# Attention and a gated feed-forward layer on one core: a V bank from the common pool, fifteen exponential tiles, a new instruction order, and a DMA queue kept in program order

## The chip, the cores and the metric

The kernel runs on one core of a Trainium2 chip. The core has TensorE (PE, matrix products into eight PSUM banks), VectorE (DVE), ScalarE (ACT), GpSimd (POOL), and SyncE (SP), which issues all the DMAs here. The metric is device time in microseconds (us) of one execution. Before the change it is 1711.22 us, the median of 3 runs (1711.19 to 1714.54). One more execution was profiled.

## What is computed

The reference, cut to its core (2048 tokens of width 512, 32 heads of width 16, a hidden width of 1792, all in float32):

```
xn = layernorm(x)
q, k, v = split(xn @ wqkv)                  # 32 heads of 16
s = softmax(q k^T * 16**-0.5) v  @ wo       # full attention
g = silu(((xn @ w_gate) * (xn @ w_up)) @ w_down)
return x + s * g
```

## The kernel before

**Attention** is cut into 32 units: a group of 4 heads by a chunk of 512 queries. A unit has 16 turns of 128 keys. For each unit the scores are formed twice. The first time (`score`, L927) queries lie on the partitions, and DVE reduces each 128x512 tile to row maxima (`mx`, L929). `maxima` and `rest` turn these into two extra rows of the query operand (through `MD` in DRAM back to `qs`). The second time (`expo`, L955) keys lie on the partitions, the extra rows subtract the maximum, and ACT takes the exponential into a tile `e` (L957). A turn gives four `e` tiles. `pv` (L966) then multiplies these by `V` into one PSUM bank that holds the unit's whole sum; `heads` transposes it on DVE (code `x`, L993), scales it (`c`), transposes it back and stores it to `OD` (`b`).

**The projections, the feed-forward layer and the output projection** are sums of 12 or 15 products (an `Out`). Operands are split into a high and a low part, so that three products stand for one in higher precision.

**Halves.** A score product has 48 or 50 rows, and each product of an `Out` is cut into two of 64 rows (L465). One lies on partitions 0 to 63, the other on 64 to 127, and two of these "halves" run at once on the two halves of the array. `pv` instead uses all 128 rows and 32 columns, four heads side by side. So PE changes between two ways of use: a stretch of halves, then a **V block** of one, two or three turns, then halves again.

**The order** of PE, ACT and DVE is written by hand in the string `ORDER`. `t`, `T` are halves for exponentials (lower, upper rows), `s`, `S` halves for maxima, each with the digit of its PSUM bank; `o` opens an `Out` in a bank, `f` and `F` are its lower and upper halves; `v`, `w`, `z` are V blocks of one, two and three turns; `l` is a tiny read by ACT after a lower half sum; `e` and `d` are evacuations of an `Out` by ACT and DVE; `X` and `k` transpose and copy tokens at the start; `m`, `r`, `x`, `c`, `b`, `h`, `y` are the steps named above and of the feed-forward layer; `Q` loads and splits attention output for the output projection. The part before `|` is the start.

**Banks.** Seven PSUM banks (digits 0 to 6) are shared by the halves through tags; the eighth, tag `pv`, belongs to `pv` alone, and a unit's first turn takes it again only when the previous unit's transposition has read it.

**Tiles.** The `e` tiles are a ring of `EBUFS` = 14. The raw copies `qr` in the early pool are a ring of 3.

**DMAs.** SP runs its DMAs in the order in which it is given them; a DMA whose data or target isn't ready holds all that are behind it. Up to `|` they are in program order, and after it the framework's scheduler orders them. `wdr` is one buffer through which parts of `w_down`, of `wo` (four, at the last feed-forward sum) and of `OD` pass to POOL to be split. In the last stage `z_out` makes output rows: it loads 512 KB of `YD` (the gate) and 512 KB of `x` into one of two "side" tiles (`hh` and `dl`) for two sums at a time, when the first of these opens; `end` (L796, L797) multiplies and adds, and stores to `out`. `kept_back` is a list of DMAs that are written a given number of `Out`s later.

Of the kernel before, what the change touches and what calls it, by code (L numbers as in the profile page):

```python
# [1129 lines left out]
```

## Time and profile before

| | |
|---|---|
| median of 3 runs | 1711.22 us |
| the profiled execution, its own time | 1711.76 us |
| span of the profile, first to last instruction | 1708.6 us |
| POOL busy | 583.7 us |
| weight loads (PEld) busy | 1089.4 us |
| DMA engines, mean busy share (queue q1) | 28.9% |
| moved by DMA | 145.80 MB, mean 85 GB/s |

The span leaves out 3.2 us of the execution that lie around the first and the last instruction. A row of the timeline gives the start, the duration, the engine, the line, the tiles (output<-inputs) and xN for the number of records merged in the row. Each `pv` product leaves two records, so a turn of four products is x8, and V blocks of one, two and three turns are x8, x16 and x24. In the groups by line the columns are busy time and mean duration, then the idle time of the engine ahead of the group and what ended it.

### The profile page before, as it was taken

How to read it: one execution, taken by the hardware profiler on the slowest of the kernel's cores; microseconds unless marked ns; L12 is line 12 of the kernel's file. 1: busy time of each engine (PE TensorE's matmuls, PEld its weight loads, DVE VectorE, ACT ScalarE, POOL GpSimd, SP SyncE). 2: the span in 40 equal slices, each digit the busy share in tenths (PEclk: the TensorE clock that was granted, in tenths of full speed). 3: DMA queues.
4: the chain of work that ended last, by engine and by line, in shares of the span. 5: the costliest groups of instructions: out<-in, count | busy, mean ns of one | idle time of the engine just before them, and what ended most of it. 6: DMA issues, size and time to landing. Idle time of an engine off the chain costs nothing.

```text
span 1708.6 us, 35418 instructions
## 1 busy us (share of the span) xinstructions
PE 1695.8 (99%) x13792; PEld 1089.4 (64%) x13792; DVE 1440.7 (84%) x2464; ACT 1221.5 (71%) x2503; POOL 583.7 (34%) x618
## 2 busy tenths in 40 slices
PE   8999999999999999999999999999999999999998
PEld 6976666666666556666666666666666666665555
DVE  7788888888898988888898888888988888888942
ACT  6257777777767777777677777776777677677783
POOL 6433334413504155053131622423235234043531
PEclk9999999999999999999999999999999999999999
DMA  6357332412223122321124211321225111022442
GB/s 207 112 205 230 146 131 98 103 29 60 61 50 83 64 84 72 53 75 48 42 94 84 87 40 42 82 56 53 84 70 113 30 60 53 22 80 71 134 129 79
DMA packets 119794, 145.80 MB, mean 85 GB/s; under 512 B 12620, under 2 KB 74060, under 8 KB 116940
## 3 DMA queue, kind: packets, MB, share of 16 engines
q1 hardware_dynamic: 119628, 143.55, 28.9%
q8 instruction: 108, 1.77, 0.4%
q14 instruction: 58, 0.48, 0.1%
HBM read 95.94 MB, written 47.45 MB: 84 GB/s over the span
## 4 chain that ended last, share of the span: by engine, by line
PE 97%; DVE 1%; POOL 1%; issue 0%; DMA 0%; ACT 0%; POOLq 0%; SPq 0%; DVEq 0%
PE b L465 37%; PE pv L966 27%; PE b L955 16%; PE b L927 15%; PE v L354 1%; PE p L354 0%; DVE mx L929 0%; DMA ks<-in_x_dram 0%; POOL dh L770 0%; PE b L332 0%; POOL y L441 0%; PE xT L317 0%; POOL hl L769 0%; ACT ks L295 0%; POOLq L1122 0%
## 5 line engine op out<-in xcount | busy, mean ns | idle before, releaser
L929 DVE TENSOR_REDUCE mx<-b 128x1 f32<-128x512 f32 x2048 | 1278.3, 683 | 186.4 <-PE b L927 99.3
L957 ACT ACTIVATE e<-b 128x512 f32<-128x512 f32 x2048 | 1084.1, 603 | 362.8 <-PE b L955 194.2
L927 PE MATMUL b<-ks,qs 48*128 48x512 f32 x2048 | 751.6, 412 | 0.0
L955 PE MATMUL b<-qs,ks 50*128 50x512 f32 x2048 | 722.4, 414 | 0.2
L966 PE MATMUL pv<-e,V 128*32 128x512 f32 x4096 | 488.4, 598 | 0.0
L955 PEld LDWEIGHTS b<-qs,ks 50*128 50x128 f32 x2048 | 342.4, 184 | 159.4 <-issue 48.6
L927 PEld LDWEIGHTS b<-ks,qs 48*128 48x128 f32 x2048 | 357.5, 184 | 131.6 <-DVE mx L929 51.0
L966 PEld LDWEIGHTS pv<-e,V 128*32 128x32 f32 x4096 | 109.0, 109 | 233.5 <-issue 223.6
L465 PE MATMUL b<-fh,w1h 64*128 64x512 f32 x504 | 199.4, 398 | 0.4 <-ACT look L500 0.4
L465 PE MATMUL b<-fl,w1h 64*128 64x512 f32 x504 | 197.4, 394 | 0.0
L465 PE MATMUL b<-fh,w1l 64*128 64x512 f32 x504 | 197.1, 393 | 0.0
L247 POOL CAST w1h<-w1r 128x512 fp32r<-128x512 f32 x60 | 36.6, 610 | 468.3 <-DMA w1r<-in_wg_dram 261.5
L465 PE MATMUL b<-fh,w0h 64*128 64x512 f32 x500 | 196.4, 395 | 0.0
L465 PE MATMUL b<-fl,w0h 64*128 64x512 f32 x500 | 195.7, 393 | 0.0
L465 PE MATMUL b<-fh,w0l 64*128 64x512 f32 x500 | 195.5, 393 | 0.0
L465 PE MATMUL b<-dh,hh 64*128 64x512 f32 x448 | 160.8, 396 | 0.0
L465 PE MATMUL b<-dh,hl 64*128 64x512 f32 x448 | 158.2, 394 | 0.0
L465 PE MATMUL b<-dl,hh 64*128 64x512 f32 x448 | 157.3, 393 | 0.0
L247 POOL CAST w0h<-w0r 128x512 fp32r<-128x512 f32 x60 | 36.6, 611 | 206.3 <-DMA w0r<-in_wu_dram 109.0
L465 PEld LDWEIGHTS b<-fh,w1h 64*128 64x128 f32 x504 | 92.9, 185 | 11.2 <-issue 2.2
L465 PEld LDWEIGHTS b<-fh,w1l 64*128 64x128 f32 x504 | 93.1, 185 | 8.8 <-issue 3.4
L465 PEld LDWEIGHTS b<-fl,w1h 64*128 64x128 f32 x504 | 93.3, 186 | 5.1 <-issue 0.8
(153 smaller groups left out, 1988.1 us busy)
## 6 DMA issues: line engine op xcount, KB each, us to landing
w1r<-in_wg_dram SPq DMA_DIRECT2D x56, 256.0 KB
w0r<-in_wu_dram SPq DMA_DIRECT2D x56, 256.0 KB
wdr<-in_wd_dram SPq DMA_DIRECT2D x56, 256.0 KB
qs<-QD SPq DMA_DIRECT2D x64, 192.0 KB
ks<-KD SPq DMA_DIRECT2D x12, 768.0 KB
KD<-hl SPq DMA_DIRECT2D x16, 512.0 KB
QD<-hl SPq DMA_DIRECT2D x16, 512.0 KB
OD<-tr SPq DMA_DIRECT2D x31, 256.0 KB
```

The lines of the kernel that those rows point to most:

```text
L247: cast = nc.gpsimd.tensor_copy(hi, raw)
L354: nc.tensor.matmul(o, l(d), r(d), start=k == d == 0, stop=k == 2 and d == ND - 1)
L465: nc.tensor.matmul(self.o, l[rows], r[rows], start=x == 0 and n == 0, stop=last and (x == 0 or self.engine is not None), skip_group_check= ...
L927: nc.tensor.matmul(o, QS[i][b:b + KB, pr, t * P:(t + 1) * P], k[b:b + KB, pr, kc * 512:(kc + 1) * 512], start=True, stop=True)
L929: nc.vector.tensor_reduce(MX[i][:, j, t, kc:kc + 1], o, axis=AX.X, op=OP.max)
L955: nc.tensor.matmul(o, k[b:b + KR, pr, kt * P:(kt + 1) * P], QS[i][b:b + KR, pr], start=True, stop=True)
L957: fst["recent"] = fst["exp"] = nc.scalar.activation(e, o, AF.Exp, scale=DH ** -0.5).ins.name
L966: nc.tensor.matmul(fst["pv"][32 * j:32 * j + 32], V[:, kt, h0:h0 + 32], es[j], start=kt == 0, stop=kt == NT - 1)
```

## The change

- `EBUFS` goes from 14 to 15.
- The bank of a unit's V sum is taken from the common pool, now eight banks (digits 0 to 7), by a new code `P` with its digit. A new unit's bank can be taken while the old one is still unread, so a V block may hold turns of two units.
- `ORDER` is new from its first line to its last.
- `order_.run(rest_of)` moves inside the context that keeps SP's queue in program order.
- The load of a side tile is put off by one `Out` (`kept_back` with 1). Of the four raw parts of `wo`, two go through the weight tiles `w1r` and `w0r` at once, and two through `wdr` one and two `Out`s later.
- The ring `qr` has 2 buffers; copies of turned tokens at the start use up to four `e` tiles instead (`turned_raw`).

No product, evacuation or transfer of data is added or taken away: 512 turns, 9508 halves, 218 `Out`s in both.

```diff
-EBUFS = 14
+EBUFS = 15
 ORDER = """
-X01o2fkX34kffkfS5fS6jfffjfS0ffS5ko1lX36jfFfFjfFfFs0FkfFfFfFufFfS5fFfFo4Fls0kX35fFfFefS0fFfFfFfFfFs0FfFfFkfFo6S2lfFfFef
+X01o2S3X45kkfS6fS7kfS0fS1fjfffjfffko4lX36jfFfFjfFfFfFkfFs7FufFfFfFfFfFo0S1lfkfS7fFfFfFfFefFfFfFfFs1FfFo5FlfFfX36efFfFkf
...
+    spare = []
+    def turned_raw():
+        if now[0]:
+            return qp.tile([P, D], F32, name="qr", bufs=2)
+        if len(spare) < 4:
+            spare.append(etile())
+        else:
+            spare.append(spare.pop(0))
+        return spare[-1]
...
-        raw = qp.tile([P, D], F32, name="qr", bufs=3)
+        raw = qp.tile([P, D], F32, name="qr", bufs=2) if hi is None else turned_raw()
...
+                elif code == "P":
+                    pvs[len(pvs)] = pool(int(next(codes)))
...
-                for d in range(ND):
-                    raw = fp.tile([P, D], F32, name="wdr", bufs=1)
+                def part(d, raw):
                     dma(raw, wo[d * P:(d + 1) * P])
                     split_rows(raw, *[t[:, d] for t in fst["w"]])
+                for d, n in enumerate(("w1r", "w0r")):
+                    part(d, wtile(n).rearrange("p d q -> p (d q)"))
+                for d in (2, 3):
+                    order_.kept_back.append([d - 1, lambda d=d: part(d, fp.tile([P, D], F32, name="wdr", bufs=1))])
...
         def begin():
             if t % 2 == 0:
-                here = fst["side"][t // 2]
-                assert not sides[t // 2]
-                dma(here[:, 0:2], YD[c][:, t:t + 2])
-                dma(here[:, 2:4], x[(4 * c + t) * P:(4 * c + t + 2) * P].rearrange("(t p) d -> p t d", p=P))
-                sides[t // 2] = 2
+                order_.kept_back.append([1, load])
+        def load():
+            here = fst["side"][t // 2]
...
     def pv(i, kt, es):
         g = i // NC
-        if kt == 0:
-            fst["pv"] = fst["banks"].tile([P, 512], F32, tag="pv", name=f"pv{i}", bufs=1)
         for j in range(4):
             h0 = (4 * g + j) * VW
-            nc.tensor.matmul(fst["pv"][32 * j:32 * j + 32], V[:, kt, h0:h0 + 32], es[j],
+            nc.tensor.matmul(pvs[i][32 * j:32 * j + 32], V[:, kt, h0:h0 + 32], es[j],
                              start=kt == 0, stop=kt == NT - 1)
...
             with tc.manual_schedule(engines=SPLITS):
                 order_.run(begin)
-        order_.run(rest_of)
+            order_.run(rest_of)
```

Where one unit ends and the next begins, PE's order before the change, at the second of these places (x4 is one turn; `pv_2476` is the old unit's sum, `pv_3186` the new one's):

```order
L966 MATMUL pv_2476<-e,V 32x512 x4
L955 MATMUL b_3161<-qs,ks_132 128x512
L955 MATMUL b_3165<-qs,ks_132 128x512
L955 MATMUL b_3169<-qs,ks_132 128x512
L465 MATMUL b_3068<-fh,w1h 128x512
L927 MATMUL b_3174<-ks_132,qs 128x512
L465 MATMUL b_3068<-fl,w1h 128x512
L955 MATMUL b_3178<-qs,ks_132 128x512
L955 MATMUL b_3182<-qs,ks_132 128x512
L966 MATMUL pv_3186<-e,V 32x512 x8
```

PE's order after the change at the third of these places, which is of a kind that the order before doesn't have (L986 is `pv`, L949 `score`, L977 `expo`, L477 a half of an `Out`; `b_3138` and `b_3845` are the V banks of two units):

```order
L977 MATMUL b_3836<-qs,ks_132 128x512
L977 MATMUL b_3840<-qs,ks_132 128x512
L986 MATMUL b_3138<-e,V 32x512 x4
L986 MATMUL b_3845<-e,V 32x512 x4
L949 MATMUL b_3863<-ks_541,qs 128x512
```

Before, two turns of two units stood in two blocks with eight halves between them; after, they stand in one block. Counted over PE's whole order, the 512 turns stand in 236 V blocks before (40 of one turn, 116 of two, 80 of three) and in 211 after (13, 95, 103).

SP's order before the change, in the last stage around the second refill of a side tile (`dl<-YD_123`); `OD_120` is attention output of the second chunk of queries, `OD_122` of the fourth:

```order
L177 DMA wdr<-OD_120 128x1x512
L177 DMA hh<-YD_123 128x1024
L177 DMA hh<-in_x_dram 128x2x512
L177 DMA dl<-YD_123 128x1024
L177 DMA dl<-in_x_dram 128x2x512
L177 DMA w1r<-OD_122 128x1x512
```

SP's order after the change, from the second refill to the third (`hh<-YD_124`):

```order
L177 DMA OD_120<-tr 128x512
L177 DMA wdr<-OD_120 128x1x512
L177 DMA dl<-YD_123 128x1024
L177 DMA dl<-in_x_dram 128x2x512
L177 DMA out_dram<-dl 128x512
L177 DMA w1r<-OD_122 128x1x512
L177 DMA w0r<-OD_122 128x1x512
L177 DMA wdr<-OD_122 128x1x512
L177 DMA wdr<-OD_122 64x1x512
L177 DMA out_dram<-dl 128x512
L177 DMA hh<-YD_124 128x1024
```

The second refill now stands behind a store of `OD_120` and a load of what was just stored, and the third behind four loads of `OD_122` of which the last two pass through the one `wdr` buffer.

More of the change, by code (lines that the diff above doesn't have):

```diff
@@ new lines @@
+FfFfS7fFfFo2S4lefS6fFfFfFs0FfFs7FfFfFmfFfFfS4fFo1S6lfS0fFfFefFfFfFrs7FfFfFs4FfFs6S0fFfFo3FlfS7efFfFs4FfFfFfFs6S0fS7fS5
+fFfFfFo2FlfFfFfFes4Fs6Fs0FfFfFs7Ft1S5fT4fFfFfT6fFfFs0Flo1es7T4t6FfFs5Ft3S0fFt4FfS7t6FfS5fT3fFs0FfT4fS7fT6fFfFs5Flt3T4s
+0Fs6FP7wet3S5t4Fs0Fs6Ft2Fs3Ft5Fo4Ft0FfFfS2fT6fS5fT3fFfS0fT6s2Fs5T3vet6S0t3T1s2S5ws0T6fS2fT3fo1S5lfT6fT0s3Ft2FfFs6Ft5Fs
+0FfFt3FfS2fT6fFs5Ft3FfS0fFfS2efS6s5T3lzs0T4s2Ft3Ft6Fs5Ft4Fo0FfFt3S2fFt6Ft5FfS4fFfS2fT3fFfS6fS4efT5ms2T3wrs6T1s4T5t3T2v
+fS6t1T5ls4S3vt2S6o1T5fS4fFfT3fS2t6Fs5Ft4FfFs3FfT2s6Ft5FfS4fFt2T3fFfFfFs6S5lt2S4wes6T3t2Fs5Ft0Fo4FfS3fT6fS2t5FfFs0FfT3s
@@ new lines @@
+6FfT2fS5fFt3FfFfFfS0et2T6ls5S3P1zxs0T2s5Fo6T3fFt7Fs2Ft0FfFs5FfT3s7FfT2fFs0Ft3FfS5fT7fS2fFfS0efT3t5S7lwcs2T4o3S0fT5fT7f
+FfS4t2FfFs0FfT5s7Ft4FfFfS2t5Fs0Ft7S4fFfFs2FfS5es0T7lzs4T6o2T7fS5fFt0FfS6fT4s7FfFt5S0fFfT6fS4t7Fs5FfFt0T6fFs4Fs7FfFt0T5
+lwebt6S4o7Fs0T5t3FfFfS6fS4t5FfT0fFfS3t6Fs5FfS4t0FfFfT3fFms6Ft0T5fFs4S3lzers6T0t5Fs4Fo2Ft3Fs0FfFs6T5fT4s3FfFfT0s5Ft6FfF
+fS4fFfS3efT0fS5fT6t4S7lwt0S3t6Fo5S7t4FfFs0Ft3Fs6Ft7FfFfS4fT0s3FfT6fS7fFfT0fFfS4s3T6fFt0S7lzext6S4o3S7fT0fS1fT2fFs4T6fF
+fT0s7Ft2Fs1FfFt6FfS4t0FfS2t7Fs6FfS1fT0t4FlP7zcs2Fs6Feo0T4fFs1FfT5fFs2T4fFfT6s5Fs1Ft4FfFt2S6fFt5FfFfS4fS1efT2s6T5lwt3S4
@@ new lines @@
+t2Fs1Fs6Ft5Fo3Ft4FfS2fT1fFfS5t6FfS4t2FfS1fFfT6fFfFbfS5es4T2ls1T6ws5T0s4Ft2Ft6Fs1Ft0Fo5FfS2fFfT4fS6s1T0fFfT2s4FfFt0S6fF
+fS1fFfS2et0T4lzmrt3S6o1S2fT0fFfT4s3FfT6fS0fT2s4FfFt3Fs6Ft0FfFs2Ft3FfFfFfS4et0T6ls2S3wt5S4t0Fs2Ft6Fo3FfS5t4FfS0t2FfFs6F
+fT5fS4fT0s2FfFfT5fFfFs6S4efS0s2T5lzs6T1s4Ft5Ft0Fs2Ft1Ft6Fs5Fo4FfS0fFfT2fS1fT5fS6fFt2T0fFfS1fS5fFt2T6lP0wexs1T2o5T6fS7f
+FfT3fS2fT1fFfS7fT6s3Ft2FfFs1Ft6Fs7Ft3Fs2FfFt6T1fFs7S3lzecs2T6s7T1o4FfFt3Fs6FfFs2T1fFfT7s3Ft6FfS1fFt2S7fFt3S6fFfFfS1efT
+2s7T3lwt5S6o1S7fT2fT3fFs5FfFt6S2t7FfS3fFt5FfS6t2FfFs7FfT3fFs5Ft2S6fFs7T3lzebs5T2s6Ft3Ft4Fo7Fs2Ft5FfFs6FfT3s4FfS2fT5fFf
@@ new lines @@
+T3fS6fT4fFfS5t2T3fFms6S4lwers5T2o3S6t1Fs4FfFt2Fs5Ft1FfFfT6s2FfT4fFs5FfT1fS6t2FfFfS4fT1fS5t6S2lwdt1S4t6Fs5Ft2Fo7FfS1t4F
+fFfS5fT6s2Ft1FfS4fFt6T5fFhfS2fFs1Fs4S6zext5S2fS1fT3o4S6lfT0fS5fT2fFt3FfS1t0FfFt2Fs6FfT3fFs5T0fS1fFt2FfFs6Flt3Fs5S0t1FP
+2zcdht3S6o5S0fT1fFt7FfS3fT6fFt1Fs0FfT7s3Ft6FfFs1FfT0s7FfFfS3efT6s1T0lws7T4s3Ft6Fo0Ft1Fs4FfFt7FfS3fT6s1Fs4FfT7fFfFfT6fS
+3t7S1fFfS4fT6zlbdht7S3s1Ft6Ft4Fo5Fs7FfT3s6FfFfT1fS4fT7fS3t6Fs1FfFt4FfS7fFfS3efT6s1T4lwmrt0S7o6S3t4FfFt1Fs0Ft7FfFfS3fT4
+fS1fFfT7fS0s3T4fFfT1fFs7Flt0Fs4Fs3T1zdhs7T0s4Ft1Fs3Ft5Fs0Ft7Ft1Fo4FfFfS5fT3fS7fT0fFfS1t3S5fFfFfS7efT0s1T3lws5T6t0Fs7Fs
@@ new lines @@
+1Ft3Ft6Fo5FfFs7FfT0fS3fFfT6fS1t0FfS7fT3fS6fFt1S0fFt7S3lP6zdhxs0T1o7S3fT4fT2fFfS1fFs0T4s3Ft2FfFt1FfS4t0FfFs2FfT3s1FfFs4
+FfS0et3S2lwct5S1o4T3fS0fT2fFfS5t1Ft3FfS0fFt2Fs5FfT1fFfT3s0FfT2fS5fT1fFs3FfFs0S2ls5Ft1Fzds3T1s0Ft2Ft5Ft7Fs1Fo3FfS2fT0fF
+fT5s1FfT7fS2fT0fFfS5t1FfS7t2FfFfS0t5Ft1Fs7S2zebs0T5fT1fS7o4lfT2fS5fT0fFt1Fs7Ft2FfS5t0FfFms1Ft7Fs2Ft5FfFfFfS0fT7s1FfT5f
+FfFfS2es0S7lzrs1T5t3Fs2Ft0Fs7Ft5Fo1Fs3Ft2FfT0fFs7FfFt5S3fT2fFfS0s7FfT5fT3fFfS2fT0fS5fS7s3Ffet2T0lzxs5T4t2Ft0T7s3Fo6Fs4
+FfFfT5fS2fT3fS0fFt7FfS4t5FfS2t3Fs0Fs7FfT4fFs5Ft2FfFht3S0lP4zect2S7s5T3o0T1fFfFfS2t7Fs3Ft5FfS1fFfT2s7FfT3s5FfFt2T1fFs7S
@@ new lines @@
+3fFfFt2S5lwes7T1o3T2fS5fFfT6fS1fT7fFfS5fT2s6Ft1FfFs7Ft2Fs5Ft6FfFs1Ft2S7fFt5S6lzbdht2S1t5S7o6T0fFfFfS2fT1fS5fFfT7fS0fT2
+s1Ft5Fs7FfFt0FfFs2Flt5Fs1Fs7T0wemrs2T5o1Fs7T0fFt3Fs5Ft2Fs0Ft7FfFfS3fT5fFfS0fT2fS7s3T5fFfFt2T0fFs7S5lzdht2S3o0T7fS5fFfS
+6t2FfFs3T7fFt5Fs2Ft6Fs7FfT3fFs5FfT2fFfFfS7et6T3ls5S2wt1S7t6Fs5Fs2Ft3Fs1Ft7Fo6FfT5fFfS3s2T7fFfFfT5fS1fT7s3FfFfT5fS2s1T7
+lP3zdhxs2T5t7Fs1Ft0Fo4Fs5FfT2fFfS1fT7fS0t5FfFs2Fs1T7fFt0FfFfS5fS2efT7s1T0lcwt6S5t7Fs2Fo0Ft1Fs6Ft5FfS7t2FfFs1Ft6FfFfS7f
+T5fS2fT6fS1fFfT5fS7t2S6lzdhs1T5t2Fs7Ft6Fo4FfS5fT1s2Ft7FfS6fFt5FfS1t2FfFs7FfT5fFfS6fS1efS2t5T7lwbt0S6o1S2fT5fFfT7fS0fT6
@@ new lines @@
+fS5fT2fFfS7fT0s6Ft5FfS2fFt0T7fFs6Fs5FfFs2Fls0Fms7Ft6Fzdrs5T6o2T0fS7fT4fFfS6fT5fS0t7FfFfS4t6FfFt5S0t7FfFt6S4fFs5T0fFfFs
+4T7fFs6Fls5Fs0Fs4T7zds6T7t5Fs0Ft4Ft1Fs7Fo6FfT5fT0fS4fFs7Ft1FfFt5FfS4t0Ft7FfS1fFfFfT5dfS4fS0fT7fS1s2T5lP4zxs0T7t5Fs1Ft2
+Ft3Fs7Fs0Fo5FfT1fFfS2fT7fT3fS0fS1fFt7S2fFfFt3T0fFfS1fS7cfFt3Flt2Fs0S1zdt3S7t2Fo0S1fFfT6s3FfT7s2FfT1t6FfFs3Ft7Fs2FfFt1F
+fS6fT3s7FfT2fFs1Ft6T3fFhs7S2lzdt6S1o3Fs7T2fFfT5fS6t1FfFfS7fT2fS5t6Fs1FfFt2Fs7FfT5s6FbfFs1T2fFs7T5lwems6T2o5T0fS1fS7fFt
+2FfS6t0FfT1fFfS2t7Fs0Ft6FfS1fFt2Frs7FfFs0T6fFt2S1lzdhs7T6t2Fs0Ft1Fo3FfS6t7FfFs0Ft2Fs1FfT6fS7fFfT2fS0t1S6fFfFfS7efS2t1T
@@ new lines @@
+0lwt5S6o1Fs7T0fFt2Fs5FfFs6T0s7FfT2fFfT5fS0fT6fS2fFt7FfFs5Ft6T0fFs2S7lP5zdhxs2T6s7Ft0Fs3Ft4Ft6Fo2FfFfS7t0FfS4fT3fFfS6fT
+0fS7t4FfFfS3s6T0fFt7S4lwect0S3s6T7t1Fo4FfFs0FfT3fFs6Ft7Fs1FfFfT3s0Fs6T7fFfFs1T3wdhs0T7t3T6s1S2vs0T7fS1s3T6vt7S2fT6fS0f
+S1o3lfT7fS2t6FfFt0FfS7t1FfS6t2FfT0fFfS7fT1s6FfFt2Fbs0Ft7FfS1ms6Flzdrs0T2o7S1fT6fFfS4fT2fFs0T6fFt1Fs2Ft4FfS6fFt0S1fFt2F
+s4FfFt0S6fFs1T2lwds4T0t2Fs6Ft1Fs3Fo0FfT4s2FfFt6Fs1Ft3FfS4fT2fS6fFfT1fFfT3dfS4fS2s6T1lws7T3t1Fs4Fo2Ft6Fs3FfS7t1FfT4fFfS
+6t3Ft1Fs7FfFfFfT4dfS6fT3fS7fT1s0S4lP3zyxt1S6o7T0s4FfFt5Fs1FfFt6Fs4T0fFfS5fFfT6fS1s4T0fFt5FfFfFs1S6efS0t4T5lwct2S1s6Ft4
@@ new lines @@
+Fs0Ft5Fs2Fo1FfT4fFs6T5fFt0FfS4fFt5FfFfT2dfS6fS0fT5fS4t7S2lzyht5S6o0T7fS4fT2fFfS5fT6fS7t4FfFt2FfS5fT6s7Ft4FfFs2Fs5FfFs7
+Fls6Ft4Ft2Fwebs5T4o7S6fT2fT1fFs4FfT5fFmfT2s6Ft1FfS4fFt5FfS2t6FyfFs1Ft5S4zrdht6S2fS1o5T4lfS0ffT6fS2t4FfFt1FfS6t0Fs4FfT2
+s1FfFt6Fs0FfT4fFfS2t6Fls1Fs4T0wyet6S2o0T7s1FfFt4Fs6FfT2s7Ft1FfFfS4fT6fS2fT7s1FfFfT6fFs4Fs2T7fFt6S1lP4zdhxt7S2o6S1t5FfT
+3fFs7FfFfT2fS1t5FfS3fFt2S7fFt1FfS5fT3fFs2Flt7Fs1Fs5T3wect7S2o1S5fT3fFs0FfT7fFs2T3fFt5Fs7Ft0Fs3FfT2fFfS5fT7s0FfFs3T2fFs
+5T7lzdhs0T2o3T7fS5fFt6FfS2fT0fFs5Ft7Fs6Ft2Fs0FfFt7S5fFs6T2fFfFfS0efT7t2S5lwbt1S6o7S0fT2fFfT5fS1fT6fFs0Ft2Fs5FfFt6S1fFt
@@ new lines @@
+2S0fFfFs5T6fFt1Fls2Fmzdhrt6S0t1Fo5S2t3FfFfS6fT0fFs2FfT1s3Ft6FfFs0Ft1Fs2FfT3fS6fFfS0efT1s2T3lws6T7s0Ft1T3o2FfFfS7fT6fS1
+t0FfFs3Ft7S6fFt1FfS0fFt7S3fFfT6s1FfFfT7fS0t6S3zdxs1T7fT6o0S3lfT5fS4fS7fT1fFt6Fs3Ft5Fs4Ft1FfFs7Ft6Fs5FfT3fFfS4t1FfS6t7F
+fFfFfS5efS3cs4T1lP7zs6T2o5T1fT3fS4fFfS2fT6fFfT1fS4t3FfFs2Ft6Fs1Ft4Fs3FfFt6Fs2Ft1FfFs4FfS3efT6t2S1zfS4o0T6lfS3fT2fT1fS4
+fFt6Fs3Ft2Fs1Ft4FfFs6Ft3FfS2t1FfFs4FfT3fS6fT2bfFfFfFs4S1les3T2t6Fzs4T5s1Ft2Ft6Fs3Ft5Fs4Fo2FfT1fFfS6s3T5fFfT4fS1fFs6T5f
+Ft3S4fFmfFt5S1fFhs3S6lzert5Fs4T0o1FfFfT3s6T5fFfT4s0FfFt3Fs6Ft5FfFfS0fT4s3FfFfS6efT5s0S4lwt2S3o6S0fT5fFt4FfS2fT3fS5t0Ff
@@ new lines @@
+Fs4Ft2Ft3FfS5fFs0Ft2S4fFfFt3T5fFt2S0lwdhxs4T3s0Fo5T2fFs1T7fFt3T4fFs2Fs0FfFt7T1fFs3FfFfS2t4T7fFfS0fS3fFs1S4leP2zct7S0t6
+Ft3S1o4FfFt7FfS0fFfT6t1FfS3fFfT7s0FfT6fFs3FfT1s7FfFs0T6lwdht1S3o7S0t6FfFfT5fS1fT3fFfS0fT6s5FfT1fFs3Ft6Fs0Ft5FfFs1Fs3Ff
+S6et0S5lzbs1T4s3Fo0T6fFt5Fs4Ft1FfFfS3fT6s5Ft4FfFs1Ft6FfFfT3dfT4fS5fS1fS6s7T3lwht4Ft3S5o1FfS6t7FfFmfT4fT5s3Ft6FfS7fFfFt
+4FfS3t5FfS7fFs6FfS4et3T5lwrs7T0s6Fo3T5fT4fFs0FfT7s5FfT6fFs4FfT0fFfS5t7S6fFt0S4fFfFt7Fls5Ft6S0zdht7S4o5S0fT6fFfFt7S1fFt
+4FfS0t6FfS7fT1fFs4FfT0s6Ft7FfFs1Ft0T4fFs6S7lP1wext0S6s7Fo4T3fFfS2fT0fFfT6s7Ft3Fs0FfFfT2s6FfT7fS3t0FfS2fFfT6fFfS7t0S3lF
@@ new lines @@
+cs2S6zds7T0t3Fs2Fs6Ft5Ft0Fs7Ft3Fo2FfFfT5fS6fT0fS7fT3fFfT5s6FfFs7T0fFt3FfS5fT6fS0s7FfS3zlds5T6t0Fs7Ft3Fo4FfS6fT5fFfT0bf
+S7fT3fT6fFfFs5Ft0FfS7t3FfFs6Ft5FfS0t7T3fFfFs6S5lzdmrs0T7t3Fs6Ft5Fs2Fo7Fs0FfT3fFt6FfS5fT2fS3fS0t6FfFfT5fFfS2t6S3fFt0S5f
+FfFt6FfS2s3T0lzds5T6s2Ft0Ft3Fs4Fo6Ft5FfS0fS2fT3fFfT4s5Ft0FfFs3Fs2T4fFs5T0fFfFt4FhfS3s2T0zdxt4S5fS3o0T2lfS7fT1fT4fS5fFs
+2Ft3Fs1Ft7Ft4FfFs5FfFt3Fs2FfT7s1FfS4fS3efT5P7wlct6S2t5Fs1Ft4Ft3Fs6Fo2Fs5FfT1s4FfFfT6s3FfT5fFfFfT1dfS4fT6fS3fS5t1S0lzht
+6S4o3S5t1Ft0FfFfS6t4Fs1FfS5fT0fFfT6s4FfFs1T0fFs5T6fFfFs4T0fFs1T6lwebs5T0s4Ft6Fo1FfS2t0FfFs5T6fFfT4fS0t2FfS6fFt5FfS4t0F
@@ L163 @@
+fFfFfFfFfFo4FlfFfFfFdfFfFfFfFfFfFfFfFwlxFFFcFbFFFFF
 """
@@ L334, in copy @@
         def copy(half, o):
-            raw = qp.tile([P, D], F32, name="qr", bufs=3)
+            raw = turned_raw()
             nc.scalar.activation(raw, o, AF.Copy)
@@ L364, in qk_proj @@
         yield from full(o, ((hi, lambda d: xh[c][:, d]), (lo, lambda d: xh[c][:, d]), (hi, lambda d: xl[c][:, d])))
-        hi, lo = qp.tile([P, D], F32R, name="hl", bufs=2), qp.tile([P, D], F32, name="qr", bufs=3).bitcast(F32R)
+        hi, lo = qp.tile([P, D], F32R, name="hl", bufs=2), qp.tile([P, D], F32, name="qr", bufs=2).bitcast(F32R)
         nc.scalar.activation(hi, o, AF.Copy)
@@ L974, in heads @@
         tn = tr.rearrange("p b e -> p (b e)")
-        pv_bank = fst["pv"]
+        pv_bank = pvs[i]
         late = i >= NU - NC
```

197 lines of the change are left out of this document (71 added, 126 removed).

## The prediction

> **What bounds the kernel now.** I read the page first (busy times, slices, chain), then the windows by stage, then PE's timeline at single blocks.
>
> ```profile
> span 1708.6 us, 35418 instructions
> PE 1695.8 (99%) x13792; PEld 1089.4 (64%) x13792; DVE 1440.7 (84%) x2464; ACT 1221.5 (71%) x2503; POOL 583.7 (34%) x618
> PEclk9999999999999999999999999999999999999999
> PE 97%; DVE 1%; POOL 1%; issue 0%; DMA 0%; ACT 0%; POOLq 0%; SPq 0%; DVEq 0%
> 0.00:50.00 50.00, 44.36 (x299) 34.66 (x301) 34.96 (x86) 30.67 (x58) 33.52 (x44) 1.00 0.59 192
> 500.00:550.00 50.00, 50.00 (x415) 30.95 (x414) 44.61 (x76) 35.75 (x75) 18.20 (x19) 1.00 0.45 88
> ```
>
> The last two rows are windows: the stretch, its length, then the busy times of PE, PEld, DVE, ACT and POOL, the granted clock, the DMA share and GB/s. PE is busy all the time but for some 13 us (1708.6 less 1695.8), of which 5.6 lie in the first 50 us; its granted clock is full; the chain of waits runs through PE for 97%. The end therefore moves only if PE's own stream gets shorter or new waits get into it. But "busy" hides how densely PE issues. That is seen at a V block:
>
> ```profile
> 117.03 0.44 PE L955 MATMUL b<-qs,ks 50*128 50x512 f32 x1
> 117.05 0.41 PE L927 MATMUL b<-ks,qs 48*128 48x512 f32 x1
> 117.40 1.92 PE L966 MATMUL pv<-e,V 128*32 128x512 f32 x16
> 119.25 0.50 PE L955 MATMUL b<-qs,ks 50*128 50x512 f32 x1
> 119.25 0.49 PE L927 MATMUL b<-ks,qs 48*128 48x512 f32 x1
> 119.59 0.40 PE L955 MATMUL b<-qs,ks 50*128 50x512 f32 x1
> 119.59 0.39 PE L927 MATMUL b<-ks,qs 48*128 48x512 f32 x1
> 119.82 0.39 PE L955 MATMUL b<-qs,ks 50*128 50x512 f32 x1
> ...
> 109.19 2.78 PE L966 MATMUL pv<-e,V 128*32 128x512 f32 x24
> 111.91 0.50 PE L927 MATMUL b<-ks,qs 48*128 48x512 f32 x1
> ```
>
> A pair of halves starts 0.23 us after the pair before it (119.59 to 119.82). A three-turn block takes 2.72 us from its start to the next pair (109.19 to 111.91), a two-turn block 1.85 (117.40 to 119.25): a turn costs 0.87 and each block about 0.11 beside its turns. Ahead of the block 0.35 pass instead of 0.23 (117.05 to 117.40), 0.12 more; the first pair behind it takes 0.34 instead of 0.23 (119.25 to 119.59), 0.11 more. So **each change between halves and a V block and back costs PE about 0.35 us** on top of its work, and all of it lies on the path.
>
> **The change, part by part.**
>
> *Fewer V blocks.* Work is the same; the order has 211 blocks instead of 236. 25 x 0.35 = **8.8 us less**. Nothing else needs to happen for this: it is PE's own time. With 0.01 us of reading error in each of the three terms it is 8 to 9.6.
>
> *The banks and the fifteenth tile.* They cost no instruction. Three-turn blocks need twelve full `e` tiles ahead of them, so what could go wrong is that ACT or DVE can't follow.
>
> ```profile
> L929 DVE TENSOR_REDUCE mx<-b 128x1 f32<-128x512 f32 x2048 | 1278.3, 683 | 186.4 <-PE b L927 99.3
> L957 ACT ACTIVATE e<-b 128x512 f32<-128x512 f32 x2048 | 1084.1, 603 | 362.8 <-PE b L955 194.2
> ```
>
> Both engines' idle time is mostly waiting for PE: 363 us ahead of ACT's exponentials, 186 ahead of DVE's maxima, 0.79 per block of the 236. DVE has the smaller reserve and it lies in the V blocks, where no scores are made; it is a rival below. Small waits between halves exist already: from 111.91 to 117.05 there are 44 halves, so 22 pairs and 21 steps, in 5.14 us; with 0.34 for the first step and 0.23 for the others they would take 4.94. So 0.2 us are lost in such a stretch, some 40 us over the some 200 long ones of the run. I take that as unchanged by the new order, with a tenth of it, 4 us, as the bound to either side.
>
> *The start.* Copies of turned tokens go through spare `e` tiles instead of `qr`. The PE idle time of the first 50 us is 5.6 us and lies in the start that the change leaves alone (the loads, the layer norm and the first transpositions). I take nothing; 1 us either way bounds it: POOL, which splits the copies, is busy for 33.5 of the 50 us there (the fifth of the busy times in the row), so it has a third of the time in reserve.
>
> *`wo` in two ways, `wdr` freed.* Two parts no longer wait for the one buffer. PE isn't shown waiting for them, so nothing.
>
> *SP in program order, later refills.* Up to the last stage the waits at SP are for things that were given out shortly before, and loads stand far ahead of use; nothing. In the last stage two refills of a side tile stand behind waits. The rows on which I price them:
>
> ```profile
> 1608.84 0.71 DVE L993 STREAM_TRANSPOSE tr<-pv 128x512 f32<-128x512 f32 x1
> ...
> 1611.24 0.23 DVE L980 RECIPROCAL rc<-tr 128x16 f32<-128x16 f32 x1
> 1611.51 0.42 DVE L981 TENSOR_TENSOR on<-tr,rc 128x256 f32<-128x256 f32 x1
> 1611.97 0.71 DVE L985 STREAM_TRANSPOSE tr<-on 128x512 f32<-128x512 f32 x1
> ```
>
> ```profile
> 1612.71 0.32 SPq L177 DMA_DIRECT2D OD<-tr  x1
> 1615.69 0.60 SPq L177 DMA_DIRECT2D wdr<-OD  x1
> 1616.34 0.58 SPq L177 DMA_DIRECT2D w0r<-OD  x1
> 1621.97 6.65 SPq L177 DMA_DIRECT2D wdr<-OD  x2
> 1629.34 0.34 SPq L177 DMA_DIRECT2D out_dram<-dl  x1
> ...
> 1662.51 0.39 SPq L177 DMA_DIRECT2D dl<-YD  x1
> ```
>
> ```profile
> 1665.00:1666.00 1.00, 1.00 (x10) 0.68 (x7) 0.00 (x0) 0.19 (x1) 0.00 (x0) 1.00 1.06 279
> 1666.00:1667.00 1.00, 1.00 (x9) 0.81 (x6) 0.00 (x0) 1.00 (x3) 0.17 (x1) 1.00 0.58 197
> 1667.00:1668.00 1.00, 1.00 (x11) 0.42 (x13) 0.00 (x0) 1.00 (x3) 0.92 (x2) 1.00 0.01 4
> ```
>
> A refill from `YD` issued at 1662.51 has landed when the traffic ends at about 1666.9: 4.4 us. *Second refill* (`dl<-YD_123`): from the V block's end, DVE's four steps take 0.71+0.23+0.42+0.71 = 2.1, the store of `OD` issues, the load of what it stored issues 3.0 later (1612.71 to 1615.69) and takes 0.6 to issue: the refill goes out 5.7 to 5.8 us after the block and lands at 10.2. DVE's `end` for it stands 42 halves and one two-turn block after: 42 x 0.117 + 1.85 + 0.35 = 7.1, and 0.4 for the last product: DVE waits 2.7. *Third refill*: the four loads of `OD_122` need 1.2 for the first two and 6.65 for the pair through `wdr` (the row of that length), the stored row 0.4 and the refill lands 4.4 later, 12.7 us behind `Q3`. `end` stands 47 halves, one two-turn and one three-turn block behind: 5.5 + 2.2 + 3.1 = 10.8. DVE waits about 1.9. Behind both waiting instructions stand DVE's maxima, whose banks PE needs; and DVE has 0.79 us of idle time per block in which to catch up. So PE loses between nothing (all is absorbed) and 4.6; I take the middle, **2.3 us more**. The other refills have waits of nothing or a few tenths by the same sum.
>
> [...]
>
> *Sum*: 1711.76 (the profiled execution's own time) - 8.8 + 2.3 = 1705.3. That execution is 0.5 us above the median of the runs shown, so **1704.7 us** for the median.
>
> **The rivals.**
>
> *A. DVE keeps its idle time.* DVE is 89% busy in the window of 500 to 550 and nearly without a pause between the V blocks. A three-turn block starves it longer. If its 186 us of idle time don't shrink with the number of blocks, DVE is the bound and gives all back at the banks: 1711. For it: longer blocks, the same seven banks to fill ahead of most of them. Against: DVE would have to lose 0.88 per block instead of 0.79, and one more bank is to be had where units change.
>
> *B. Slower by the queue.* The place is the last stage. If the refills land 5 us or more behind their `end` at three places, and the score rows of the last unit (`MD`) stand behind them, PE stands for all of it: 15 us against 8.8, so 1711.2 + 6 = 1717. It decides from 12 us of new waits. For it: the single wait of 6.65 us, in a queue that can't go around it. Against: my sums give 2 to 3 us a place, and the work left to DVE there is small.
>
> *C. All the gain and more.* The refill waits are absorbed, and a fifth of the small waits goes as the eighth bank loosens the reuse: 1711.2 - 8.8 - 3 = 1699.5.
>
> *D. The change doesn't do what it says.* If PE broke the joined blocks up again, nothing would be saved, 1711. PE runs in its written order, and the rows of the order show the joined blocks, so I give this no chance of its own.
>
> **How the numbers follow.** Forecast 1704.7: 0.60, with its own range of 1701 to 1708.5 (0 to 4.6 at the refills, some of the small waits). C 1699.5: 0.18. A 1711: 0.14. B 1717: 0.08. The range takes in C's and the forecast's, and A's up to its price: 1698 to 1711.5; what is left out is B and the outer parts of A and C. About 0.2% (3.4 us) is what a measurement of this kernel can tell from no change, so faster means below 1707.8 and slower above 1714.6. Faster: C and all but a little of the forecast, 0.77; within: A and that little, 0.15; slower: B, 0.08.
>
> **What would show it.** V blocks in PE's timeline: 211, a two-turn one still 1.85 us from its start to the next pair, the pair behind it 0.34. If DVE's idle time ahead of L929's successor falls by some 9 us, A is out; if it stays at 186 and weight loads of scores wait longer for DVE, A is right. In the last stage a wait of DVE's `end` for a DMA of 2 to 3 us at the second and third refill shows my step on SP right; none shows C, and three of 5 us or more B. The prediction is wrong if PE's pairs in the middle of the run step at other than 0.23 to 0.24, or if the first V block begins more than 1 us earlier or later than at 109.2.

## The result and the profile after

The changed kernel takes 1721.4 us (median of 4 runs, 1719.96 to 1722.63) against 1711.2 us before (4 runs, 1710.42 to 1714.54): a ratio of **1.0055, 95% interval 1.0043 to 1.0067**. It is slower by 10 us, where 1704.7 was forecast. The profiled execution took 1719.96 us with a span of 1718.0. In the experiments below, one execution of the run with the third refill's letter (2040.2 us, at a mean granted clock of 0.75 where its other nine have 0.996 or more) is left out of its median.

The page of the changed kernel, in the order in which the page of before was read (busy times, granted clock by slices, chain, and the group of DVE's maxima with busy time, mean and the idle time before them):

```profile
span 1718.0 us, 35374 instructions
PE 1695.7 (99%) x13792; PEld 1089.8 (63%) x13792; DVE 1430.0 (83%) x2464; ACT 1224.3 (71%) x2503; POOL 583.4 (34%) x618
PEclk9999999999999999999999999999999999999989
PE 95%; DMA 2%; DVE 1%; issue 1%; POOL 0%; ACT 0%; SPq 0%; POOLq 0%; DVEq 0%
L951 DVE TENSOR_REDUCE mx<-b 128x1 f32<-128x512 f32 x2048 | 1267.8, 683 | 194.4 <-PE b L949 100.1
```

PE is busy for the same time, the span is 9.4 us longer, the last but one slice has a lower clock, and the chain now runs through DMAs for 2%. PE's list of waits (sum, times, longest) names the DMAs and their place:

```profile
PE b L949 <- DVE hh L814: 7.0, 1, 7.0
PE b L949 <- DVE dl L814: 2.6, 1, 2.6
...
PE b L949 <- DMA qs<-QD: 1.8, 2, 0.9
```

None of these three is in the list of before. The two `L814` are `end`, the multiplication in front of an output row, so the first two lines are refills of a side tile; the third is a load of queries. In PE's timeline (start, length, then what ended the idle time) the four stalls are the gaps between one pair of halves and the next:

```profile
180.56 0.39 PE L477 MATMUL b<-xl,w1h 64*128 64x512 f32 x1
181.83 0.47 PE L949 MATMUL b<-ks,qs 48*128 48x512 f32 x1 [0.88 <-DMA qs<-QD]
...
1574.06 0.40 PE L477 MATMUL b<-dh,hl 64*128 64x512 f32 x1
1575.38 0.46 PE L949 MATMUL b<-ks,qs 48*128 48x512 f32 x1 [0.93 <-DMA qs<-QD]
...
1612.16 0.39 PE L477 MATMUL b<-fh,w1l 64*128 64x512 f32 x1
1615.13 0.50 PE L949 MATMUL b<-ks,qs 48*128 48x512 f32 x1 [2.57 <-DVE dl L814]
...
1632.92 0.40 PE L477 MATMUL b<-fh,dh 64*128 64x512 f32 x1
1640.27 0.79 PE L949 MATMUL b<-ks,qs 48*128 48x512 f32 x1 [6.95 <-DVE hh L814]
```

From start to start they are 1.27, 1.32, 2.97 and 7.35 us, where a step takes 0.23: 1.0 + 1.1 + 2.7 + 7.1 = **12.0 us** of new stalls. The last pair runs for 0.79 instead of 0.39, at a granted clock of 0.50 (window of 1640 to 1641). Windows of 1 us behind the third stall (busy times of PE, PEld, DVE, ACT and POOL, the granted clock, DMA share, GB/s) show how long that lasts:

```profile
1615.00:1616.00 1.00, 0.87 (x6) 0.51 (x8) 1.00 (x3) 0.10 (x1) 0.31 (x2) 1.00 0.04 14
1616.00:1617.00 1.00, 1.00 (x6) 0.93 (x7) 1.00 (x3) 0.57 (x2) 1.00 (x1) 0.51 0.07 16
1617.00:1618.00 1.00, 1.00 (x8) 0.88 (x7) 0.46 (x1) 1.00 (x2) 0.18 (x1) 0.50 0.00 0
1618.00:1619.00 1.00, 1.00 (x8) 0.92 (x6) 0.69 (x1) 0.32 (x2) 0.00 (x0) 0.50 0.79 270
1619.00:1620.00 1.00, 1.00 (x9) 0.92 (x8) 0.92 (x2) 0.80 (x2) 0.00 (x0) 0.79 0.39 66
```

Here the clock falls after PE has resumed, pairs step by 0.43 instead of 0.23 (1617.06 to 1617.49), and 0.49 + 0.50 + 0.50 + 0.21 = 1.7 us of full speed are gone. In the fourth stall it falls at 1636.5, while PE stands, and comes back at 1646.7; from PE's start at 1640.27 the same sum gives 3.2 us. So the stalls cost 12.0 us, and **4.9 more by the clock**.

To see whether the saving came, I set both traces beside each other at equal work: every matmul record counts with its usual step (0.1145 us for a half, 0.109 for one of `pv`), and the changed kernel's time is read where it has done as much as the kernel before.

| time in before, us | after less before, us | V blocks more or fewer so far | what is left without 0.35 us per block |
|---|---|---|---|
| 200 | +1.8 | +2 | 1.1 |
| 1000 | -1.5 | -7 | 1.0 |
| 1500 | -3.2 | -18 | 3.1 |
| 1600 | -3.2 | -20 | 3.8 |
| 1620 | +0.3 | -24 | 8.7 |
| 1660 | +10.2 | -24 | 18.6 |
| 1700 | +9.5 | -25 | 18.2 |

The saving follows the blocks (25 x 0.35 = 8.8); what is left grows by 14.8 us between 1600 and 1660, as much as the third and fourth stall (9.9) and the clock (4.9) take. It ends at 18.2, of which stalls and clock are 16.9. Why the third and fourth stall are so long stands in SP's queue (start and length of each issue) and in POOL's rows at that time:

```profile
1606.56 0.38 SPq L177 DMA_DIRECT2D OD<-tr  x1
1608.85 0.61 SPq L177 DMA_DIRECT2D wdr<-OD  x1
1609.51 0.45 SPq L177 DMA_DIRECT2D dl<-YD  x1
...
1617.21 0.34 SPq L177 DMA_DIRECT2D out_dram<-dl  x1
1617.59 0.60 SPq L177 DMA_DIRECT2D w1r<-OD  x1
1618.24 0.58 SPq L177 DMA_DIRECT2D w0r<-OD  x1
1618.91 9.39 SPq L177 DMA_DIRECT2D wdr<-OD  x2
1635.08 0.34 SPq L177 DMA_DIRECT2D out_dram<-dl  x1
1635.46 0.43 SPq L177 DMA_DIRECT2D hh<-YD  x1
```

```profile
1631.88 0.60 POOL L787 CAST w0h<-wdr 64x512 fp32r<-64x512 f32 x1 [4.12 <-PE b L986]
...
1633.80 1.25 POOL L815 TENSOR_TENSOR dl<-dl 128x512 f32<-128x512 f32 x1
```

The two loads through the one buffer `wdr` make a row of 9.4 us, because the second goes out only at 1627.8, when POOL has split the first. POOL splits the second load at 1631.88 and only then makes the add of `end` (L815). The store `out<-dl` waits for that add until 1635.08, and the refill `hh<-YD` stands behind the store. (The releaser that the first POOL row names, `PE b L986`, is only the last event before; what POOL waits for is this second load. In the first run below, where the second load is issued later, the same pause is 4.12 us long and ends by `wdr<-OD`.) The refill goes out 17.9 us after the first raw load (`w1r<-OD`, 1617.59), where 8.3 had been reckoned.

### The profile page after: what moved, and what is told of

The parts are those of the page before. It is cut to its first block, busy times and chain, and to the rows that moved or that the text cites. A ratio compares the mean times of both kernels' runs of the same rounds, so it can differ in the third digit from the quotient of the medians.

```text
span 1718.0 us, 35374 instructions
## 1 busy us (share of the span) xinstructions
PE 1695.7 (99%) x13792; PEld 1089.8 (63%) x13792; DVE 1430.0 (83%) x2464; ACT 1224.3 (71%) x2503; POOL 583.4 (34%) x618
## 4 chain that ended last, share of the span: by engine, by line
PE 95%; DMA 2%; DVE 1%; issue 1%; POOL 0%; ACT 0%; SPq 0%; POOLq 0%; DVEq 0%
PE b L477 37%; PE b L986 27%; PE b L977 16%; PE b L949 15%; PE v L366 1%; DMA qs<-QD 0%; DVE mx L951 0%; DMA hh<-in_x_dram 0%; PE p L366 0%; DMA dl<-YD 0%; DMA ks<-in_x_dram 0%; DMA wdr<-OD 0%; DMA hh<-YD 0%; POOL w0l L788 0%; PE xT L329 0%
## 5 line engine op out<-in xcount | busy, mean ns | idle before, releaser
L949 PE MATMUL b<-ks,qs 48*128 48x512 f32 x2048 | 760.7, 412 | 11.3 <-DVE hh L814 7.0
L977 PE MATMUL b<-qs,ks 50*128 50x512 f32 x2048 | 765.6, 415 | 0.0
L986 PE MATMUL b<-e,V 128*32 128x512 f32 x4096 | 484.1, 598 | 0.0
L949 PEld LDWEIGHTS b<-ks,qs 48*128 48x128 f32 x2048 | 362.8, 185 | 157.1 <-DVE mx L951 40.6
L977 PEld LDWEIGHTS b<-qs,ks 50*128 50x128 f32 x2048 | 358.6, 185 | 148.5 <-issue 39.4
L986 PEld LDWEIGHTS b<-e,V 128*32 128x32 f32 x4096 | 111.6, 109 | 236.7 <-issue 231.3
L477 PE MATMUL b<-fh,w1h 64*128 64x512 f32 x504 | 198.2, 396 | 0.0
L477 PE MATMUL b<-fl,w1h 64*128 64x512 f32 x504 | 198.1, 395 | 0.0
L477 PE MATMUL b<-fh,w1l 64*128 64x512 f32 x504 | 197.6, 394 | 0.0
L477 PE MATMUL b<-fh,w0h 64*128 64x512 f32 x500 | 197.3, 395 | 0.0
L477 PE MATMUL b<-fl,w0h 64*128 64x512 f32 x500 | 196.7, 395 | 0.0
L477 PE MATMUL b<-fh,w0l 64*128 64x512 f32 x500 | 195.4, 393 | 0.0
L477 PE MATMUL b<-dh,hh 64*128 64x512 f32 x448 | 160.4, 394 | 0.0
L477 PE MATMUL b<-dl,hh 64*128 64x512 f32 x448 | 160.2, 394 | 0.0
L477 PE MATMUL b<-dh,hl 64*128 64x512 f32 x448 | 159.6, 393 | 0.0
L477 PEld LDWEIGHTS b<-fh,w1h 64*128 64x128 f32 x504 | 93.0, 186 | 8.4 <-issue 2.4
L477 PEld LDWEIGHTS b<-fh,w0h 64*128 64x128 f32 x500 | 92.8, 186 | 6.5 <-issue 1.3
L477 PEld LDWEIGHTS b<-fh,w1l 64*128 64x128 f32 x504 | 93.2, 186 | 5.5 <-issue 1.7
```

What stands on the lines that cost most here:

```text
L477: nc.tensor.matmul(self.o, l[rows], r[rows], start=x == 0 and n == 0, stop=last and (x == 0 or self.engine is not None), skip_group_check= ...
L949: nc.tensor.matmul(o, QS[i][b:b + KB, pr, t * P:(t + 1) * P], k[b:b + KB, pr, kc * 512:(kc + 1) * 512], start=True, stop=True)
L977: nc.tensor.matmul(o, k[b:b + KR, pr, kt * P:(kt + 1) * P], QS[i][b:b + KR, pr], start=True, stop=True)
L986: nc.tensor.matmul(pvs[i][32 * j:32 * j + 32], V[:, kt, h0:h0 + 32], es[j], start=kt == 0, stop=kt == NT - 1)
```

## The experiments

The theory: fewer V blocks save their 8.8 us, and waits in SP's program order take more than that back. The rivals: longer blocks, the floating bank and the fifteenth tile cost time by themselves; program order costs everywhere; the clock falls for another reason.

### One letter: the second refill

```diff
 (ORDER)
-...7S3Q5o6T1fF...
+...7S3o6Q5T1fF...
```

> Only the place of one letter in the order table is changed: the raw rows of OD_120 are asked for right behind the refill of pair 1 (dl<-YD_123) instead of ahead of it, so that this refill no longer stands in the queue behind a load that waits for a store. Theory (the loss lies in the refills that stand behind waits in SP's queue, and in the clock that falls behind each stall): DVE's wait of 3.2 us for dl<-YD, the PE gap of 3.0 us at 1612 and the stretch of clock 0.50 behind it are gone, the gap of 7.4 us near 1633 stays: 1721.4 less 3 to 6, 1715 to 1718. Rival (longer V blocks or the floating bank cost the time, the refill is only where the wait is seen): PE stands at the same place for another releaser, 1720 to 1722.

Measured: 1721.5 us, ratio 1.0057 (1.004 to 1.0073). The gap at 1612 is gone and the time is the same: the theory's place was right and its number wrong. Of the two refill waits in PE's list only one is left, and it has taken over the other's time (11.4 us, where the two were 2.6 and 7.0); SP's rows show why:

```profile
PE b L949 <- DVE hh L814: 11.4, 1, 11.4
```

```profile
1618.73 0.60 SPq L177 DMA_DIRECT2D w1r<-OD  x1
...
1620.07 9.40 SPq L177 DMA_DIRECT2D wdr<-OD  x2
1636.22 0.34 SPq L177 DMA_DIRECT2D out_dram<-dl  x1
1636.61 0.42 SPq L177 DMA_DIRECT2D hh<-YD  x1
```

The third refill goes out at 1636.6, 1.1 us later than in the changed kernel, because its chain begins with a raw load (`wdr<-OD`) that now lands behind the refill: POOL begins to split it at 1615.10 instead of 1613.25, and so the add, the store and the four loads behind it are later too. What PE gains at 1612 it waits at 1630. The chain, not PE, sets when this place is passed.

### The other letter: the third refill

```diff
 (ORDER)
-...S5s0FQ3lt2T3wdt2S1t3Fs5Ft0Fs6Ft2Fo1FfS3...
+...S5s0Flt2T3wdt2S1t3Fs5Ft0Fs6Ft2Fo1Q3FfS3...
```

> Only the place of the other letter: the raw rows of OD_122 are asked for behind the refill of pair 2 (hh<-YD_124) instead of ahead of it. Theory: the wait of 9.4 us of DVE's end for hh<-YD and the PE gap of 7.4 us are gone, with the 3 us that the lowered clock cost behind it, the gap of 3 us at 1612 stays: 1721.4 less 9 to 11, 1710.5 to 1712.5. Rival (the blocks or the bank): no change, 1720 to 1722. Rival (the clock falls of itself at this time, not because PE stood): the gap goes but the clock of 0.50 between 1640 and 1646 stays, 1713 to 1714.5.

Measured: 1713.7 us, ratio 1.0009 (1.0 to 1.0019); 7.7 us less than the changed kernel instead of 9 to 11. The long wait is gone, and the wait at the second refill stays, as expected (the first line). Two smaller ones have come in: one for a later refill, and one for the rows of maxima (`qs<-MD`), which stand in the queue behind the same pair of raw loads (now 11.3 us long, 1626.9 to 1638.3):

```profile
PE b L949 <- DVE dl L814: 2.8, 1, 2.8
...
PE b L977 <- DMA qs<-MD: 1.5, 1, 1.5
...
PE b L977 <- DVE dl L814: 0.7, 1, 0.7
```

The rival that blocks or bank cost the time falls: PE's blocks and banks are the same here.

### All refills at once

```diff
-                order_.kept_back.append([1, load])
+                load()
```

> The new kernel, but a refill of a side tile is written at once when the first Out of its pair opens, as in the kernel before, instead of one Out later; the queue stays in program order. Theory: all refills stand ahead of the waiting loads, both stalls of PE are gone and the clock stays full; the 8.8 us of fewer V blocks remain: 1702 to 1705. Rival (program order of SP costs as such, by loads of queries that leave later): the two refill stalls go but something else is late, 1706 to 1711. Rival (blocks or bank): 1718 or more.

Measured: 1718.4 us, ratio 1.0038 (1.0023 to 1.0053), far from 1702 to 1705. Both refill stalls are gone, and one of 7.5 us has come (and one of 1.9 us for an exponential):

```profile
PE b L977 <- DMA qs<-MD: 7.5, 1, 7.5
```

```profile
1623.25 11.37 SPq L177 DMA_DIRECT2D wdr<-OD  x2
1635.35 0.34 SPq L177 DMA_DIRECT2D out_dram<-dl  x1
1642.40 0.34 SPq L177 DMA_DIRECT2D out_dram<-hh  x1
...
1643.81 0.56 SPq L177 DMA_DIRECT2D MD<-mt  x1
1648.82 0.55 SPq L177 DMA_DIRECT2D qs<-MD  x2
```

DVE had `mt` ready at 1635.85. Its store goes out 8.0 us later, behind a store of `out` that waits until 1642.40 and a refill of 1 MB, and its way back (`qs<-MD`) is issued 5.0 us after it; at the unit before it was 2.0 (1587.56 to 1589.53 in the changed kernel). Whatever stands behind the raw loads pays; the refills were only the first in line.

### The queue back to the scheduler

```diff
-            order_.run(rest_of)
+        order_.run(rest_of)
```

> The new kernel, but after the start the DMA queue is again put in order by the scheduler, as in the kernel before; the program on PE, ACT and DVE is the same to the instruction. Theory: the refills are drawn ahead of the waiting loads, so it gains what the early refills gain, and the two waits for qs<-QD (0.9 us) go as well: 1701.5 to 1705. Rival (the loss is of the order on PE, ACT and DVE, not of the queue): 1718 to 1722.

Measured: 1713.95 us, ratio 1.0012 (1.0002 to 1.0021): 7.4 us gained by the queue alone, with PE, ACT and DVE the same to the instruction. So at least 7.4 us of the loss are the queue's. But it isn't the 1701.5 to 1705 that I expected: the scheduler's queue with the later refills has waits of its own (in PE's list 2.5 us for `qs<-MD`, 2.8 for POOL's splits at three places, 1.5 for copies by ACT).

### A second buffer

```diff
-                   fst["fp"].tile([P, D], F32, name="wdr", bufs=1))
+                   fst["fp"].tile([P, D], F32, name="g" if (c, d) == (NC - 1, ND - 1) else "wdr", bufs=1))
```

> The new kernel with one edit: the last raw rows of OD_122 land in the tile g instead of wdr, so SP's row of 9.4 us (the second load of a pair through one buffer) goes. Theory (refill 3 stands behind the store of out, that behind POOL's add, and that behind POOL's splits, which wait for the second load): POOL's four splits run without a pause, the store goes out about 4 us earlier and DVE's wait for hh<-YD falls from 9.4 to about 5: 1716 to 1718.5. Rival 1 (only SP's wait on the buffer holds the refill): the refill goes out at about 1620 and no wait is left, 1709 to 1711. Rival 2 (the wait at SP is covered by others): 1720 to 1722.

Measured: 1717.4 us, ratio 1.0033 (1.0021 to 1.0045), 4 us less than the changed kernel. SP's row of 9.4 us is gone, yet the refill stays behind the store that waits for POOL, as the theory has it. From `w1r<-OD` (1621.93) to `hh<-YD` (1635.65) it is 13.7 us instead of 17.9, and DVE's wait is 5.0:

```profile
1639.67 0.69 DVE L814 TENSOR_TENSOR hh<-b,hh 128x512 f32<-128x512 f32 x1 [4.98 <-DMA hh<-YD]
```

Rival 1, that only SP's wait on the buffer holds the refill, falls.

### Both letters, the second buffer, and earlier queries

```diff
 (ORDER: both letters as above; the buffer g as above)
-        if kt == 8 and i + 2 < NU:
+        if kt == (1 if i == NU - 3 else 4) and i + 2 < NU:
             load_q(i + 2)
```

> Both letters moved as in the two runs with one letter each (refills of pair 1 and pair 2 go out ahead of the raw rows), the last raw rows of OD_122 land in the free tile g so that SP doesn't wait there for POOL's split, and the loads of queries (qs<-QD) are written at the fifth round of a unit (the second one of unit 29) instead of the ninth. The program on PE, DVE and ACT is that of the new kernel but for what the two letters move. Theory (the waits in SP's program order ate the gain, one taking the place of the other): from 1714.0 of the run with the letter Q3 moved, less the waits that its trace shows (1.0 at 182 us, 1.1 at 1576, 2.9 at 1616, 1.7 and 0.9 at 1644 and 1649): 1706.4, range 1703 to 1709; faster than the kernel before. Rival (a late stage with the new order has no slack and a new wait comes for each one removed): 1711 to 1716.

Measured: 1708.8 us, ratio **0.9982 (0.9974 to 0.9991)**: 12.6 us less than the changed kernel, and faster than the kernel before. It ends at the upper edge of what was expected, as one wait of 2.2 us is left, again for the rows of maxima (and one of 0.5 for the second refill):

```profile
PE b L977 <- DMA qs<-MD: 2.2, 1, 2.2
```

```profile
1636.45 0.34 SPq L177 DMA_DIRECT2D out_dram<-hh  x1
1636.89 0.56 SPq L177 DMA_DIRECT2D MD<-mt  x1
```

`mt` was ready at 1631.2. The store `out<-hh` ahead of it waits for POOL's add, and that for POOL's splits.

### What a block costs

On top of the last kernel, 41 blocks are broken in two by putting the pair of halves ahead of a block inside it; work and the order on DVE, ACT and SP stay.

```diff
 (ORDER, one of 41 places; s2S5 are two halves, w two turns)
-...s2S5w...
+...vs2S5v...
```

> As e5_fix, but 41 V blocks of two or three turns are broken in two by putting the pair of halves ahead of the block between its first turn and the rest; the work, and the order on DVE, ACT and SP, are the same. My price of 0.35 us per change between halves and a block and back: e5_fix plus 14.4 us (13 to 16). Rival (part of the price is idle time of PE that DVE's or ACT's pace sets, and that comes back elsewhere): plus 0 to 8.

Measured: 1723.4 us, 14.5 above the kernel without the breaks: 0.35 us a block. PE's own busy time takes it:

```profile
PE 1706.7 (99%) x13792; PEld 1083.2 (63%) x13792; DVE 1431.9 (83%) x2464; ACT 1224.4 (71%) x2503; POOL 584.2 (34%) x618
```

It was 1692.0 without the breaks, 14.7 less, with the same 13792 matmuls. DVE and ACT don't give any of it back.

### Program order in the kernel before

```diff
-        order_.run(rest_of)
+            order_.run(rest_of)
```

> The kernel before with one line of the change: the DMA queue in program order to the end. Order of work, banks, tiles and refills as before. Rival of the theory (program order as such costs, by 5 us or more, whatever the order table): 1716 or more. Theory (it costs only where a refill or a row of maxima stands behind a load that waits, and the old order opens the refill at the first Out of a pair): 1711 to 1715.

Measured: 1727.0 us, ratio 1.0086 (1.0072 to 1.01). The rival is right here: with the old order table, program order costs 15 us. It costs it at three places, where a load of queries or a refill stands behind a store that waits (PE's list of waits):

```profile
PE b L927 <- DMA qs<-QD: 4.7, 2, 2.9
PE b L465 <- DVE hh L796: 4.1, 1, 4.1
```

Behind each of the three the clock stands at 0.50 for 3.4 us (from 138.0, 889.0 and 1643.3), so another 1.7 us are gone each time. At equal work the loss is 4.7 us by 150, 9.2 by 1450 and 14.7 by 1640, flat between. So it isn't a price per DMA but one per place at which a due transfer stands behind one that waits, and such places are in the middle of the run too. The new order table has fewer of them.

### The rows of maxima

On top of the kernel with both letters, the second buffer and earlier queries, one add is done by DVE instead of POOL.

```diff
-LEAD = 21
+LEAD = 22
```

> e5_fix with LEAD 22 instead of 21: one add of end (the second hh before the maxima of the last unit) is done by DVE instead of POOL, so the store of out in front of MD<-mt no longer waits behind POOL's splits, which wait for PE. In e5_fix the rows mt were there at 1631.2 and MD<-mt left only at 1636.9; PE then waited 2.2 us for qs<-MD (gap of 2.6) and its clock stood at 0.50 for some 3.4 us (1.7 lost). Theory: MD<-mt leaves at 1631.2, the gap and the lowered clock go: 1708.8 less 4, 1705 (1703.5 to 1706.5). Rival (a new wait takes its place): 1707 to 1709.

Measured: 1705.6 us, ratio 0.9963 (0.9951 to 0.9976). The store no longer holds `MD<-mt`, which leaves as soon as `mt` is there (1632.81); the wait for `qs<-MD` is gone, and one of 1.6 us for the second refill is the only one left in this stage (the clock stands at 0.50 for 3.4 us behind it, from 1612.6, which is another 1.7 us):

```profile
1628.28 0.34 SPq L177 DMA_DIRECT2D out_dram<-hh  x1
1632.84 0.56 SPq L177 DMA_DIRECT2D MD<-mt  x1
```

### The second refill alone, earlier

On top of the last kernel, one refill is written at once.

```diff
-                order_.kept_back.append([1, load])
+                if (c, t) == (0, 2):
+                    load()
+                else:
+                    order_.kept_back.append([1, load])
```

> As e9_maxrows, and the refill of pair 1 alone (dl<-YD_123) is written when its pair opens, ahead of the second store out<-hh. In e5_fix DVE's end waited 1.2 us for it and PE 0.5 (gap of 0.9). Theory: that gap goes, 0.5 to 0.9 below e9_maxrows, 1704.3. Rival (the refill's own wait for the side tile sets it): the same as e9_maxrows to 0.3.

Measured: 1704.3 us, ratio **0.9956 (0.9942 to 0.9969)**, the best of all; the wait for the second refill is gone from PE's list. It is 17.0 us less than the changed kernel, and 7.3 less than the kernel before beside it. In the stage where the changed kernel lost its time, PE now stands for 0.04 of 60 us, at full clock:

```profile
1600.00:1660.00 60.00, 59.96 (x480) 33.19 (x477) 34.97 (x59) 49.05 (x103) 25.37 (x26) 1.00 0.35 117
```

## Why the prediction was wrong

**Fewer V blocks: right.** 8.8 us were forecast. A two-turn block still takes 1.86 us from its start to the next pair (108.33 to 110.19, the first one). The table at equal work shows them, and 41 breaks cost 14.5 us against 14.4 reckoned with the same 0.35.

**Banks, tile, DVE's idle time (rival A): right to leave out.** With the stalls gone, the same order of blocks runs in 1704.3 us, so DVE doesn't give the saving back. The sign that I had named for rival A misled: the idle time ahead of the maxima rose from 186 to 194 us, and in that kernel without the stalls it is still 192, so the stalls don't explain it and its cause stays open. The other half of the sign spoke against rival A: weight loads of scores waited 51.0 us for DVE's maxima before, 40.6 in the changed kernel and 39.3 in the kernel without the stalls.

**Waits at SP up to the last stage, "nothing": wrong by 2.1 us.** Two loads of queries arrived 0.9 us late. I argued that loads stand far ahead of use. The new queue issues these at 177.59 and 1571.11, only 4.2 and 4.3 us before PE goes on with them: the first right behind a store of queries, the second behind a part of `wo` that waits until POOL has emptied `wdr` (1570.7). That second one is also a price of "`wo` in two ways", which I had put at nothing.

**The refills, "2.3 us more": this is the step that failed.** The DVE wait at the second refill was sized about right (2.7 forecast, 3.2 measured; the refill landed 10.2 us behind the block, as summed), but I let PE lose only half, since the maxima would catch up; PE stood for 2.7. At the third refill I forecast 1.9 us of DVE's time and 9.4 were measured. The sum counted SP's own rows between `Q3` and the refill, 1.2 + 6.65 + 0.4 (and left out the 0.4 for the last product that the second sum has, which would have made 1.5 of the 1.9). It left out that the store in the middle waits for POOL, that POOL splits the raw rows ahead of the add which the store needs, and that the second split waits for the second load. The row of 6.65 was read as a length when it was a wait for another engine; in the changed kernel it became 9.4, and the store came 6.8 us behind its end.

**The clock, not in the sum at all:** 4.9 us.

Together 2.1 + 9.9 (2.74 and 7.12 at the refills) + 4.9 = 16.9 us where 2.3 stood. Rival B was the right mechanism at the right place, with a price of 15 us and a limit of 12, and I gave it 0.08; even so, only one of its three places had a wait of 5 us or more. What spoke against it, "my sums give 2 to 3 us a place", was the very sum in doubt; a chain of three queues had been summed along one of them.

What stays open: 1704.3 is 1.5 us above 1711.6 - 8.8 (the kernel before took 1711.6 beside it). The profiled execution of that kernel (1705.0 us) shows a loss of this size at the end: the clock stands at 0.50 for 3.4 us from 1693.4, while PE makes its last products, where the kernel before has full clock:

```profile
1694.00:1695.00 1.00, 1.00 (x4) 0.81 (x4) 0.26 (x1) 0.00 (x0) 0.00 (x0) 0.50 0.00 0
```

That is 1.7 us. The fastest of the five executions, 1702.67 us, has a mean clock of 0.999 where the others have 0.998, as it would without this stretch, but it was not profiled. In the changed kernel 1.3 us of the 18.2 are neither stalls nor clock. No run took these apart. Nor was it shown what the scheduler's queue would give together with the mended places.
